# Splitting float64 weights with TensorE sums in a fused Fourier, channel-mix and expert kernel

## The chip, the cores and the metric

The kernel runs on one core of a Trainium2 chip. A core has five engines that take their instructions from queues of their own, in order: TensorE (PE, with its weight loads shown apart as PEld), VectorE (DVE), ScalarE (ACT), GpSimd (POOL) and SyncE (SP, which issues transfers here). The metric is the time of one execution in microseconds (us), the median of several runs.

## The reference

```
x = fft(fft(x, axis=1), axis=2).real                 # x: 4 x 3072 x 256, float32
x_prev = x one position back (zeros first)
xk = mu_k * x + (1 - mu_k) * x_prev ; xr likewise with mu_r
k = relu(xk @ w_k) ; v = (k * k) @ w_v ; r = sigmoid(xr @ w_r)
x = r * v                                            # w_k 256x1024, w_v 1024x256, w_r 256x256
# then a mixture of 8 experts over the 12288 rows, top one, capacity 384 each:
expert = argmax(x @ w_gate); the first 384 rows of each expert go through
y = relu(disp @ w1) @ w2, times the gate's weight; all other rows of the output are zero
```

`w_k`, `w_r` and `w_v` arrive as float64, because a float32 array was multiplied by a float64 scalar. The kernel gets them as pairs of 32-bit words and must make from them a high and a low part, whose three cross products stand for a float32 product on TensorE.

## The kernel before

The first batch goes through a two-dimensional Fourier transform before anything else can run ("the start"). It has three stages. Stage 1 has seven steps (`s1`): VectorE folds each step's inputs (four additions or subtractions), TensorE multiplies by a table in float32, ScalarE copies the result out of PSUM, and SP stores it to a scratch array `fd` in memory. `turn_round` then loads it back across partitions into tiles `tin` (`tload`, L362). Stage 2 (`s2`, L371) makes eight products from those tiles, stage 3 (`s3`, L397) eight more. Each leaves through ScalarE (L392, L418), and the stage 3 results through two or more VectorE operations (L428 to L436) into the transform `X`. Stages 2 and 3 are 16 units in a fixed order, 2 of stage 2 first and then alternating.

Beside the start stands the preparation of the weights: eight blocks of 128x512, five of `w_k` and `w_r` together and the rest three of four of `w_v`'s (`split64`, L762). Each block is loaded by SP as 512 KB of words, then takes four integer operations on VectorE (L769 to L772), an addition on GpSimd (L773), a copy to the high part (L774, on ScalarE, for `w_v` on VectorE) and a subtraction on GpSimd (L775). Between the units of stages 2 and 3 the loop in the main body runs three of these steps (`STEPS`); the rest of `w_v` is prepared in the first chunk (`more_v`, `VSTEPS`). Before stage 2, 36 matmuls on zeros keep TensorE running (`keep_warm`, `WARM`).

After that follow chunks of 512 positions (`chunk`, L624). A chunk has eight steps f: six matmuls of `mm_k` (L508), and from the fourth step on six of `mm_v` for the step three back, which reads block f // 2 of `w_v`. The third step also has the twelve matmuls of `mm_r`. ScalarE takes relu and square, and makes `kh` (L518, in chunk 0 for f < 4); VectorE makes `kl` (L519). What the matmuls read is made by `mix_part` (L463): ScalarE, VectorE, ScalarE, VectorE. The next batch's Fourier transform is spread over the chunks of the current one, from a plan written out by hand (`lay`, L954); the first two stage 1 steps of batch 1 are done in the start, in float32 (`EARLY`). All engines' orders are written out by hand, with no scheduler (`manual_schedule`).

At the end, the experts run.

Of the kernel before, what the change touches and what calls it, by code (L numbers as in the profile page):

```python
# [10 lines left out]
F32 = mybir.dt.float32  # L11
# [9 lines left out]
P = 128  # L21
# [82 lines left out]
def fourier_channel_mix_moe(  # L104
# [40 lines left out]

    tri = wts.tile([P, P], BF16, name="tri")
    ones = wts.tile([P, P], BF16, name="ones")
    gm = wts.tile([P, KD, P + E], F32, name="gm")
# [8 lines left out]
    d3 = [wts.tile([P, 2, 2, P], F32R, name=f"d3{h}") for h in range(2)]  # L157
    wk = [[wts.tile([P, KD, DFF], F32R, name=f"wk{f}{h}") for h in range(2)] for f in range(2)]
    wr = [[wts.tile([P, KD, D], F32R, name=f"wr{f}{h}") for h in range(2)] for f in range(2)]
    wv = [wts.tile([P, KF, D], F32R, name=f"wv{h}") for h in range(2)]  # L160
# [56 lines left out]
    def fft_buffers(pool, tag, nx, ns, nt, ng, nv, plain=False, keep=None):  # L217
# [19 lines left out]
        (s, w, d, h): fft.tile([P, CH], F32R, name=f"x{s}{w}{d}{h}")  # L237
        for w in range(2) for s in range(w + 1) for d in range(KD) for h in range(2)
    }


    def fft_units(b, bufs, table=None, between=lambda g: None, count=0, wait=0):

# [71 lines left out]
        def s1(j):  # L315
# [32 lines left out]

            later(wait, store) if wait and j < count else store()

# [20 lines left out]
        def s2(i):  # L371
            h = turns[i]
            ps = psm.tile([P, CH], F32, name="pm")
            w = UQ * HG * UC
            for t in range(2):
                for k in range(HG):
                    o = ps[:, w * t + UQ * UC * k:w * t + UQ * UC * (k + 1)]
                    z = h == 0 and k == 0
                    nc.tensor.matmul(
                        o, tins[i % NTI][:, k, t], m2[:, HG * h + k].rearrange("p u s -> p (u s)"),  # L380
                        start=True, stop=not z, skip_group_check=z,
                    )
# [11 lines left out]
            if i + NTI < NH:  # L394
                between(i + NTI)

# [47 lines left out]
        def turn_round():  # L444
            for g in range(NTI):
                tload(g)
            for g in range(NTI):
                between(g)

# [327 lines left out]

# [4 lines left out]

    def stage(k):
        raw = spare(k) if k < 2 else stg.tile([P, CH, 2], I32, name="raw", bufs=3)
        return raw, stg.tile([P, CH], I32, name="sa", bufs=3)

    def prep_r():
        src = words(ins["w_r"]).rearrange("(d p) n -> p d n", p=P)
        return split64(src, *(t.rearrange("p d n -> p (d n)") for t in wr[0]), *stage(4))

    def prep_k(d, h):
        src = words(ins["w_k"])[d * P:(d + 1) * P, 2 * CH * h:2 * CH * (h + 1)].rearrange("p (a n) -> p a n", a=1)
        return split64(src, *(t[:, d, CH * h:CH * (h + 1)] for t in wk[0]), *stage(2 * h + d))

    def prep_v(k):
        src = words(ins["w_v"])[2 * k * P:(2 * k + 2) * P].rearrange("(f p) n -> p f n", p=P)
        return split64(
            src, *(t[:, 2 * k:2 * k + 2].rearrange("p f n -> p (f n)") for t in wv),
            spare(k % 2), spare(2).rearrange("p n w -> p (n w)")[:, CH * (k % 2):CH * (k % 2 + 1)], nc.vector.tensor_copy,
        )  # L800

# [14 lines left out]
    with tc.manual_schedule():  # L816
        with tc.tile_pool(name="stg", bufs=2) as stg:
# [6 lines left out]
            def keep_warm(n):  # L824
# [17 lines left out]
            more["s"] = []  # L842
            pk = []

            preps = [
                lambda: prep_k(0, 0), lambda: prep_k(1, 0), prep_r,
                lambda: prep_k(0, 1), lambda: prep_k(1, 1), lambda: prep_v(0),
            ]

            held = []  # L850

            def prepare(steps):

                pk.extend(steps[:5] + held)
                held[:] = steps[5:]

            def between(g):
                if preps:
                    prepare(preps.pop(0)())

# [6 lines left out]
            )  # L867
            units = fft_units(0, more, t3, between, len(CSTEPS))
# [19 lines left out]
            )  # L888
            for k in ("mu_k", "mu_r"):
                v = ins[k].rearrange("(d o) -> d o", o=1)  # L890
                for d in range(KD):
                    nc.scalar.dma_start(mu[k, 0][:, d:d + 1], v[d * P:(d + 1) * P])
                    flipped(mu[k, 1][:, d:d + 1], v, d)
            do(units, len(CSTEPS))
            for u in range(UQ):
                rs = slice(2 * FC * u, 2 * FC * (u + 1))
                nc.scalar.dma_start(m2[rs, :, u], ins["c_m2"][rs].rearrange("r (g n) -> r g n", n=UC))
            nc.scalar.dma_start(mz, ins["c_mz"])
            nc.scalar.dma_start(t3.rearrange("p v t k -> p (v t k)"), ins["c_d3"])
            keep_warm(WARM)  # L900
            parts(d1, d1f)
            parts(d3, t3)
            units1 = fft_units(1, fbuf, None, lambda g: None, EARLY, 4)
            for n in range(len(units)):
                do(units)
                if n < 3:
                    keep_warm(2)
                do(pk, STEPS[n])
                if n == 13:
                    do(units1)  # L910
                if n == 10:
                    do(units1)
                    prepare(prep_v(1))
                    for k in ("mu_k", "mu_r"):
                        for f in range(2):
                            nc.vector.tensor_scalar(mu[k, f, 1], mu[k, f], -1.0, 1.0, op0=ALU.mult, op1=ALU.add)
# [8 lines left out]
            settle()  # L925
            do(pk, STEPS[-1])
            prepare(prep_v(2))
            pv = pk + held
# [3 lines left out]
            nc.sync.dma_start(ident, ins["c_ident"])  # L932
        mp = mix.enter_context(tc.tile_pool(name="mp", bufs=1))

        def more_v(f):
# [299 lines left out]
```

## Time and profile before

| what | value |
|---|---|
| time, median of 3 runs | 642.57 us (641.83 to 643.2) |
| the profiled execution's own time | 644.52 us |
| its span, first to last instruction | 642.7 us |
| mean granted TensorE clock | 0.957 |
| PE busy | 593.9 us, 92% |
| VectorE busy | 423.2 us, 66% |
| ScalarE busy | 353.1 us, 55% |
| GpSimd busy | 149.1 us, 23% |

The page's slices of 16 us, in tenths of busy time:

```profile
PE   5855889999999999999999999999988989999992
PEld 2553667888888888888788888889978989999992
DVE  5379899966666666699757665756665746655620
ACT  2131837666565656676556566566636745655630
POOL 7246256030202022240302030202221101111121
PEclk7877797999999999999999999999998989999997
DMA  7583598242108000152421061000107645555200
```

Each digit is the busy share of one of 40 equal slices; 9 is 90% or more. PEclk is the clock granted to TensorE. TensorE is full from the seventh slice on; the first six are the start and the first chunk.

### The profile page before, as it was taken

The numbers are of one execution on the slowest core, as the hardware profiler recorded it, in microseconds if no ns is written. First come the engines' busy times: TensorE is split into PE (matmuls) and PEld (weight loads), VectorE is DVE, ScalarE is ACT, GpSimd is POOL, SyncE is SP. The second block draws the span as 40 slices with busy tenths as digits, with TensorE's granted clock in tenths as the row PEclk, the third lists the DMA queues.
The fourth block names the chain that finished last, engine by engine and source line by source line (L and its number), as shares of the span: only waits on it lengthen the run. The fifth ranks groups of instructions, "written<-read, shape, count | busy, mean of one in ns | idle before, by whom it ended". The sixth has DMA issues, their size and how long they took to land. (4 is left out here: it accounts for less than half of the span.)

```text
span 642.7 us, 9640 instructions
## 1 busy us (share of the span) xinstructions
PE 593.9 (92%) x3386; PEld 516.9 (80%) x3387; DVE 423.2 (66%) x921; ACT 353.1 (55%) x685; POOL 149.1 (23%) x195
## 2 busy tenths in 40 slices
PE   5855889999999999999999999999988989999992
PEld 2553667888888888888788888889978989999992
DVE  5379899966666666699757665756665746655620
ACT  2131837666565656676556566566636745655630
POOL 7246256030202022240302030202221101111121
PEclk7877797999999999999999999999998989999997
DMA  7583598242108000152421061000107645555200
GB/s 241 154 252 111 161 337 287 86 154 93 61 15 291 1 25 11 60 163 101 134 93 36 9 208 48 7 1 3 56 11 236 213 149 181 161 161 173 66 26 26
DMA packets 57183, 73.98 MB, mean 115 GB/s; under 512 B 8020, under 2 KB 43073, under 8 KB 57126
## 3 DMA queue, kind: packets, MB, share of 16 engines
q1 hardware_dynamic: 48610, 59.46, 29.0%
q0 software_dynamic: 5936, 13.37, 6.3%
q10 hardware_dynamic: 2580, 0.44, 0.5%
q8 instruction: 29, 0.48, 0.3%
q14 instruction: 28, 0.23, 0.1%
HBM read 43.27 MB, written 33.91 MB: 120 GB/s over the span
## 5 line engine op out<-in xcount | busy, mean ns | idle before, releaser
L488 PE MATMUL pk<-x,wk 128*128 128x512 f32 (+2 forms) x672 | 172.0, 392 | 3.4 <-ACT x L211 3.0
L488 PEld LDWEIGHTS pk<-x,wk 128*128 128x128 f32 x672 | 120.5, 192 | 25.1 <-ACT x L211 3.3
L488 PE MATMUL pv<-kh,wv 128*128 128x512 f32 (+2 forms) x448 | 134.6, 382 | 1.1 <-issue 0.6
L180 POOL DMA_INDIRECT disp<-rows,slot x50 | 53.2, 1064 | 271.5 <-ACT tmp L478 87.4
L514 ACT ACTIVATE rk<-pk 128x512 f32<-128x512 f32 (+2 forms) x112 | 64.4, 575 | 86.5 <-PE pk L488 75.1
L518 DVE CAST kh<-rk 128x512 fp32r<-128x512 f32 (+2 forms) x108 | 46.5, 430 | 91.4 <-ACT rk L515 89.7
L488 PEld LDWEIGHTS pv<-kh,wv 128*128 128x128 f32 x448 | 83.0, 189 | 17.9 <-POOL wv L775 1.3
L488 PE MATMUL pv<-kl,wv 128*128 128x512 f32 (+2 forms) x224 | 85.6, 382 | 0.0
L519 DVE TENSOR_TENSOR kl<-rk,kh 128x512 fp32r<-128x512 f32 (+2 forms) x112 | 75.5, 674 | 5.7
L1136 PE MATMUL pd<-w,h 128*128 128x256 f32 x576 | 72.8, 283 | 0.0
L1136 PEld LDWEIGHTS pd<-w,h 128*128 128x128 f32 x576 | 72.0, 192 | 0.0
L515 ACT ACTIVATE rk<-rk 128x512 f32<-128x512 f32 (+2 forms) x112 | 68.2, 609 | 3.6
L1085 DVE TENSOR_TENSOR w<-raw,w 128x512 fp32r<-128x512 f32 x60 | 41.0, 685 | 41.4 <-ACT w L1084 41.4
L180 POOL DMA_INDIRECT out<-res,ids x24 | 23.6, 983 | 121.8 <-ACT res L1143 107.7
L488 PEld LDWEIGHTS pv<-kl,wv 128*128 128x128 f32 x224 | 42.4, 189 | 8.0
L1127 DVE SCALAR_TENSOR_TENSOR h<-pk,h 128x384 fp32r<-128x384 f32 x64 | 35.3, 551 | 14.7 <-ACT h L1126 14.5
L1143 ACT ACTIVATE res<-pd,g 128x256 f32<-128x256 f32 x24 | 11.4, 476 | 54.5 <-PE pd L1136 53.2
L211 ACT CAST x<-tmp 128x512 fp32r<-128x512 f32 (+2 forms) x56 | 32.7, 585 | 14.4 <-DVE tmp L479 14.2
L488 PE MATMUL pk<-x,wr 128*128 128x512 f32 (+2 forms) x168 | 38.7, 379 | 0.0
L1084 ACT CAST w<-raw 128x512 fp32r<-128x512 f32 x60 | 36.7, 613 | 0.0
L212 DVE TENSOR_TENSOR x<-tmp,x 128x512 fp32r<-128x512 f32 (+2 forms) x56 | 36.6, 656 | 0.0
L488 PEld LDWEIGHTS pk<-x,wr 128*128 128x128 f32 x168 | 30.7, 188 | 6.0
(184 smaller groups left out, 895.8 us busy)
## 6 DMA issues: line engine op xcount, KB each, us to landing
raw<-in_w SPq DMA_DIRECT2D x60, 256.0 KB
out<-blank SPq DMA_DIRECT2D x24, 512.0 KB
tin<-fd SPq DMA_DIRECT2D x22, 208.0 KB
xin<-in_x SPq DMA_DIRECT2D x15, 256.0 KB
fd<-f SPq DMA_DIRECT2D x14, 256.0 KB
disp<-blank SPq DMA_DIRECT2D x6, 530.0 KB
d<-disp SPq DMA_DIRECT2D x8, 397.5 KB
X<-in_w_v SPq DMA_DIRECT2D x4, 512.0 KB
```

Of the source, the lines that this page charges most:

```text
L180: i = nc.gpsimd.indirect_dma_start(out=dst, out_offset=bass.IndirectOffsetOnAxis(ap=idx, axis=0), in_=src, in_offset=None, bounds_check=la ...
L211: nc.scalar.copy(hl[0], src)
L212: later(n, lambda: nc.vector.tensor_tensor(hl[1], src, hl[0].bitcast(F32), op=ALU.subtract))
L488: nc.tensor.matmul(ps, w[a][:, k, m0:m0 + P], xs[c], start=(first and n == 0), stop=(last and n == 2),)
L514: nc.scalar.activation(r, ps, AF.Relu)
L515: nc.scalar.activation(r, r, AF.Square)
L518: nc.vector.tensor_copy(kh, r) if i or f > 3 else nc.scalar.copy(kh, r)
L519: nc.vector.tensor_tensor(kl, r, kh.bitcast(F32), op=ALU.subtract)
L1084: nc.scalar.copy(h, r)
L1085: nc.vector.tensor_tensor(l, r, h.bitcast(F32), op=ALU.subtract)
L1127: nc.vector.scalar_tensor_tensor(hl, ps, 0.0, hh.bitcast(F32), op0=ALU.max, op1=ALU.subtract)
L1136: nc.tensor.matmul(ps, hs[a][:, f, t * P:(t + 1) * P], w[c][:, f], start=(f == 0 and n == 0), stop=(f == KF2 - 1 and n == 2),)
```

## The change

Of each weight block the words now go through four VectorE operations, which leave a rounded-down float32 (`a`) and two words whose upper 16 bits are read as bf16. ScalarE copies `a` to the high part. TensorE sums four products into PSUM: the identity by `a` in float32, the negated identity by the high part, and two small multiples of the identity by the two bf16 views, whose columns lie 8 bytes apart. ScalarE copies the sum to the low part. GpSimd has no part in it. `first()` holds the VectorE operations and the copy, `rest()` the matmuls and the last copy.

The words of `w_k` and `w_r` are loaded from ScalarE's queue, one block after each of five steps of stage 1, and the stage 2 tables are loaded there too, after the third step. Two blocks are split before stage 2, between three runs of zeros (18, 6 and 10 matmuls); a third is begun there; that one and two more are finished beside stages 2 and 3. Eight `tin` tiles are held, so `turn_round` issues all eight loads at once. Of `w_v` the loads of two blocks are issued late in stage 3, the first is begun after the mixing, and all four are finished in chunk 0 at f = 1, 3, 4 and 6. Batch 1's first two stage 1 steps move into the chunks, with three products instead of a float32 one, and so do the mixing of `xr` for chunk 0 and the splitting of two Fourier tables. Some tiles lie in a pool that opens after the start.

```
-EARLY = 2
-STEPS = (4,) + (3,) * 11 + (3, 0, 0, 0, 0, 0, 2)
-VSTEPS = (2, 3, 4, 4, 4, 4, 4, 4)
-WARM = 36
+WARM = (18, 6, 10)
...
-    def split64(src, hi, lo, raw, a, copy=nc.scalar.copy):
-        nc.sync.dma_start(raw.rearrange("p (a n) w -> p a (n w)", a=src.shape[1]), src)
+    def split64(queue, pool, src, hi, lo, raw, a):
+        queue.dma_start(raw.rearrange("p (a n) w -> p a (n w)", a=src.shape[1]), src)
         lw, hw = raw[:, :, 0], raw[:, :, 1]
+        le, he = (raw.bitcast(BF16)[:, :, k] for k in (1, 3))
         v = a.bitcast(F32)
         vec = nc.vector
-        return [
-            lambda: vec.tensor_scalar(a, hw, 3, 0x3FFFFFF8, op0=ALU.logical_shift_left, op1=ALU.bitwise_and),
-            lambda: vec.scalar_tensor_tensor(hw, hw, -0x40000000, a, op0=ALU.bitwise_and, op1=ALU.bitwise_or),
-            lambda: vec.scalar_tensor_tensor(a, lw, 29, hw, op0=ALU.logical_shift_right, op1=ALU.bitwise_or),
-            lambda: vec.tensor_scalar(lw, lw, 28, 1, op0=ALU.logical_shift_right, op1=ALU.bitwise_and),
-            lambda: nc.gpsimd.tensor_tensor(a, a, lw, op=ALU.add),
-            lambda: copy(hi, v),
-            lambda: nc.gpsimd.tensor_tensor(lo, v, hi.bitcast(F32), op=ALU.subtract),
-        ]
+        def rest():
+            ps = pool.tile([P, CH], F32, name={id(psk): "pk", id(psm): "pm"}[id(pool)])
+            terms = (ident, v), (neg_i, hi), (ulp_i, le), (negulp_i, he)
+            for n, (w, y) in enumerate(terms):
+                nc.tensor.matmul(ps, w, y, start=(n == 0), stop=(n == len(terms) - 1), skip_group_check=True)
+            nc.scalar.copy(lo, ps)
+        def first():
+            vec.tensor_scalar(a, hw, 3, 0x3FFFFFF8, op0=ALU.logical_shift_left, op1=ALU.bitwise_and)
+            vec.scalar_tensor_tensor(a, hw, -0x40000000, a, op0=ALU.bitwise_and, op1=ALU.bitwise_or)
+            nc.scalar.copy(hi, v)
+            vec.tensor_scalar(hw, a, -0x800000, None, op0=ALU.bitwise_and)
+            vec.scalar_tensor_tensor(lw, lw, 9, hw, op0=ALU.logical_shift_right, op1=ALU.bitwise_or)
+        return first, rest
...
-            more = fft_buffers(stg, "a", 0, 0, 1, 2, 0, plain=True)
+            more = fft_buffers(stg, "a", 0, 0, NU // (UQ * HG) - len(fbuf["t"]), 2, 0, plain=True)
...
+            nc.scalar.dma_start(ident, ins["c_ident"])
...
-            keep_warm(WARM)
-            parts(d1, d1f)
-            parts(d3, t3)
-            units1 = fft_units(1, fbuf, None, lambda g: None, EARLY, 4)
+            behind = {
+                0: lambda: weights((0, 0)), 1: lambda: weights((1, 0)), 2: tables, 3: lambda: weights("r"),
+                4: lambda: nc.scalar.dma_start(t3.rearrange("p v t k -> p (v t k)"), ins["c_d3"]),
+                5: lambda: weights((0, 1)), 6: lambda: weights((1, 1)),
+            }
+            mus()
+            for j in range(len(CSTEPS)):
+                do(units)
+                behind.get(j, lambda: None)()
+            for t, k in ((neg_i, -1.0), (ulp_i, 2.0 ** -20), (negulp_i, -(2.0 ** -20))):
+                nc.scalar.activation(t, ident, AF.Copy, scale=k)
+            do(units)
+            pw[0, 0][0]()
+            keep_warm(WARM[0])
+            pw[0, 0][1]()
+            pw[1, 0][0]()
+            keep_warm(WARM[1])
+            pw[1, 0][1]()
+            keep_warm(WARM[2])
+            pw["r"][0]()
+            units1 = fft_units(1, fbuf)
+            beside = {
+                1: pw[0, 1][0], 3: pw["r"][1], 4: pw[1, 1][0], 6: pw[0, 1][1], 7: one_less_mu, 9: pw[1, 1][1],
+                10: lambda: pv.append(prep_v(0)), 11: lambda: pv.append(prep_v(1)), 12: lambda: do(units1),
+            }
             for n in range(len(units)):
                 do(units)
                 if n < 3:
                     keep_warm(2)
-                do(pk, STEPS[n])
+                beside.get(n, lambda: None)()
             settle()
             mix_part(0, 0)
             mix_part(0, 1)
-            do(units1, EARLY)
             settle()
-            do(pk, STEPS[-2])
-            mix_part(0, 2)
-            mix_part(0, 3)
+            pv[0][0]()
...
         def more_v(f):
-            do(pv, VSTEPS[f])
+            if f == 0:
+                parts(d1, d1f)
+                parts(d3, t3)
+            if f in (1, 3, 4, 6):
+                k = (1, 3, 4, 6).index(f)
+                pv[k][1]()
+                if k < 2:
+                    pv.append(prep_v(k + 2))
+                if k < 3:
+                    pv[k + 1][0]()
             if f == 1:
-                pv.extend(prep_v(3))
...
```

## Rows read from the trace of the kernel before

**Rows 1.** Windows: stretch, its length, busy us of PE, PEld, DVE, ACT, POOL; clock, DMA share, GB/s.
```profile
29.90:41.00 11.10, 4.85 (x37) 4.21 (x36) 5.67 (x9) 2.75 (x6) 1.33 (x1) 0.87 0.94 285
41.00:55.00 14.00, 10.21 (x56) 9.08 (x56) 13.72 (x25) 4.57 (x11) 8.75 (x8) 0.86 0.64 195
55.00:69.30 14.30, 8.23 (x20) 6.03 (x21) 13.55 (x26) 4.06 (x9) 9.09 (x8) 0.51 0.25 76
...
92.50:103.50 11.00, 7.63 (x20) 5.18 (x20) 10.41 (x17) 7.38 (x13) 5.62 (x4) 0.69 1.01 369
103.50:160.00 56.50, 55.87 (x305) 47.01 (x304) 44.98 (x97) 35.71 (x65) 12.58 (x18) 1.00 0.41 133
```
**Rows 2.** Timeline of TensorE: start us, us, engine, line, what, [idle before it and releaser].
```profile
15.15 1.10 PE L333 MATMUL pm<-X,d1f 128*128 128x258 f32 x4 [0.76 <-ACT tmp L344]
...
21.74 8.36 PE L828 MATMUL pk<-busy 128*128 128x512 bf16 x37
29.94 1.03 PE L379 MATMUL pm<-m,tin 128*128 128x100 f32 x8
...
41.05 2.00 PE L379 MATMUL pm<-m,tin 128*128 128x100 f32 x8 [6.30 <-DMA tin<-fd]
...
44.16 1.43 PE L379 MATMUL pm<-m,tin 128*128 128x100 f32 x8
...
47.21 0.84 PE L410 MATMUL pm<-Ga,rows 128*128 128x192 f32 x4
...
60.12 1.65 PE L410 MATMUL pm<-Ga,rows 128*128 128x192 f32 x4 [1.21 <-DVE X L428]
66.12 3.75 PE L333 MATMUL pm<-xin,d1f 128*128 128x258 f32 x8 [4.36 <-issue]
69.31 5.87 PE L488 MATMUL pk<-x,wk 128*128 128x512 f32 x18
...
92.54 0.63 PE L488 MATMUL pk<-x,wk 128*128 128x512 f32 x2
...
97.04 1.89 PE L488 MATMUL pk<-x,wk 128*128 128x512 f32 x3 [3.02 <-ACT x L211]
...
101.28 2.36 PE L488 MATMUL pk<-x,wk 128*128 128x512 f32 x6
103.47 0.62 PE L488 MATMUL pv<-kh,wv 128*128 128x512 f32 x2
...
107.60 2.91 PE L488 MATMUL pk<-x,wr 128*128 128x512 f32 x12
110.35 0.88 PE L333 MATMUL pm<-xsp,d 128*128 128x258 f32 x6
```
**Rows 3.** Groups by line, VectorE, 29.9 to 69.3 us: count, busy us, mean ns, idle before.
```profile
L770 DVE SCALAR_TENSOR_TENSOR raw<-raw,sa 128x512 int32<-128x512 int32 x3 | 4.4, 1469 | 0.1
...
L771 DVE SCALAR_TENSOR_TENSOR sa<-X 128x512 int32<-128x512 int32 x2 | 1.4, 693 | 0.1
L772 DVE TENSOR_SCALAR raw<-raw 128x512 int32<-128x512 int32 x3 | 1.3, 428 | 0.1
```
**Rows 4.** Groups by line, GpSimd, the same stretch.
```profile
L775 POOL TENSOR_TENSOR wk<-sa,wk 128x512 fp32r<-128x512 f32 x4 | 5.9, 1479 | 0.0
```
**Rows 5.** Timeline of ScalarE's and SP's work and queues at four places.
```profile
22.01 4.08 ACTq L897 DMA_DIRECT2D m<-in_c_m  x4
...
66.13 0.32 ACT L418 COPY oa<-pm 128x192 f32<-128x192 f32 x1 [5.62 <-DVE X L434]
...
74.72 0.59 ACT L514 ACTIVATE rk<-pk 128x512 f32<-128x512 f32 x1
...
78.21 6.81 SPq L941 DMA_DIRECT2D disp<-blank  x6
```
**Rows 6.** Windows of stage 1 (columns of rows 1).
```profile
2.75:13.75 11.00, 6.43 (x16) 3.39 (x15) 6.31 (x12) 1.17 (x2) 9.35 (x26) 0.71 0.94 316
13.75:25.00 11.25, 8.82 (x33) 4.95 (x33) 6.89 (x16) 2.62 (x5) 3.94 (x20) 0.83 0.35 126
```

More of the change, by code (lines that the diff above doesn't have):

```diff
@@ L146, in fourier_channel_mix_moe @@
     tri = wts.tile([P, P], BF16, name="tri")
+    neg_i = wts.tile([P, P], F32R, name="neg_i")
+    ulp_i, negulp_i = (wts.tile([P, P], BF16, name=f"ulp{k}") for k in range(2))
     ones = wts.tile([P, P], BF16, name="ones")
@@ L157, in fourier_channel_mix_moe @@
     d3 = [wts.tile([P, 2, 2, P], F32R, name=f"d3{h}") for h in range(2)]
-    wk = [[wts.tile([P, KD, DFF], F32R, name=f"wk{f}{h}") for h in range(2)] for f in range(2)]
-    wr = [[wts.tile([P, KD, D], F32R, name=f"wr{f}{h}") for h in range(2)] for f in range(2)]
+    wk = [[wts.tile([P, KD, DFF], F32R, name=f"wk0{h}") for h in range(2)]]
+    wr = [[wts.tile([P, KD, D], F32R, name=f"wr0{h}") for h in range(2)]]
     wv = [wts.tile([P, KF, D], F32R, name=f"wv{h}") for h in range(2)]
@@ L237, in fourier_channel_mix_moe, with late_buffers, fft_units @@
         (s, w, d, h): fft.tile([P, CH], F32R, name=f"x{s}{w}{d}{h}")
-        for w in range(2) for s in range(w + 1) for d in range(KD) for h in range(2)
+        for s, w in ((0, 1),) for d in range(KD) for h in range(2)
     }
-    def fft_units(b, bufs, table=None, between=lambda g: None, count=0, wait=0):
+    def late_buffers(pool):
+        for w, n, name in ((wk, DFF, "wk"), (wr, D, "wr")):
+            w.append([pool.tile([P, KD, n], F32R, name=f"{name}1{h}") for h in range(2)])
+        for s, w in ((0, 0), (1, 1)):
+            for d in range(KD):
+                for h in range(2):
+                    xbuf[s, w, d, h] = pool.tile([P, CH], F32R, name=f"x{s}{w}{d}{h}")
+    def fft_units(b, bufs, table=None, count=0):
         xv = x[b].rearrange("(a c) n -> a c n", c=NC)
@@ L347, in store @@
                 nc.sync.dma_start(fd[:, place[j]:place[j] + n], f)
-            later(wait, store) if wait and j < count else store()
+            store()
         def load_zero():
@@ L781, in spare, with half @@
         return sp[:, 2 * CH * k:2 * CH * (k + 1)].rearrange("p (n w) -> p n w", w=2)
-    def stage(k):
-        raw = spare(k) if k < 2 else stg.tile([P, CH, 2], I32, name="raw", bufs=3)
-        return raw, stg.tile([P, CH], I32, name="sa", bufs=3)
+    def half(k):
+        return spare(2).rearrange("p n w -> p (n w)")[:, CH * k:CH * (k + 1)]
     def prep_r():
         src = words(ins["w_r"]).rearrange("(d p) n -> p d n", p=P)
-        return split64(src, *(t.rearrange("p d n -> p (d n)") for t in wr[0]), *stage(4))
+        hl = (t.rearrange("p d n -> p (d n)") for t in wr[0])
+        return split64(nc.scalar, psk, src, *hl, stg.tile([P, CH, 2], I32, name="raw", bufs=1), stg.tile([P, CH], I32, name="sa", bufs=3))
     def prep_k(d, h):
         src = words(ins["w_k"])[d * P:(d + 1) * P, 2 * CH * h:2 * CH * (h + 1)].rearrange("p (a n) -> p a n", a=1)
-        return split64(src, *(t[:, d, CH * h:CH * (h + 1)] for t in wk[0]), *stage(2 * h + d))
+        raw = stg.tile([P, CH, 2], I32, name=f"raw{d}{h}", bufs=1)
+        return split64(
+            nc.scalar, psk, src, *(t[:, d, CH * h:CH * (h + 1)] for t in wk[0]), raw, stg.tile([P, CH], I32, name="sa", bufs=3)
+        )
     def prep_v(k):
         src = words(ins["w_v"])[2 * k * P:(2 * k + 2) * P].rearrange("(f p) n -> p f n", p=P)
[L797 to L800, printed above, removed]
+        hl = (t[:, 2 * k:2 * k + 2].rearrange("p f n -> p (f n)") for t in wv)
+        return split64(nc.sync, psm, src, *hl, spare(k % 2), half(k % 2))
     def flip_weights():
@@ L842, in fourier_channel_mix_moe @@
             more["s"] = []
[L843 to L859, printed above, removed]
             one = len(CSTEPS) - 2
@@ L867, in fourier_channel_mix_moe @@
             )
-            units = fft_units(0, more, t3, between, len(CSTEPS))
+            units = fft_units(0, more, t3, len(CSTEPS))
             do(units, 2)
             keep_warm(8)
+            nc.scalar.dma_start(ident, ins["c_ident"])
             nc.gpsimd.iota(neg, pattern=[[-P, KD]], base=D, channel_multiplier=-1)
@@ L888, in fourier_channel_mix_moe @@
             )
[L889 to L897, printed above, removed]
@@ L898, in fourier_channel_mix_moe, with tables @@
-            nc.scalar.dma_start(mz, ins["c_mz"])
-            nc.scalar.dma_start(t3.rearrange("p v t k -> p (v t k)"), ins["c_d3"])
-            keep_warm(WARM)
-            parts(d1, d1f)
-            parts(d3, t3)
-            units1 = fft_units(1, fbuf, None, lambda g: None, EARLY, 4)
+            def tables():
+                for u in range(UQ):
+                    rs = slice(2 * FC * u, 2 * FC * (u + 1))
+                    nc.scalar.dma_start(m2[rs, :, u], ins["c_m2"][rs].rearrange("r (g n) -> r g n", n=UC))
+                nc.scalar.dma_start(mz, ins["c_mz"])
@@ new lines, in mus, with weights @@
+            def mus():
+                for k in ("mu_k", "mu_r"):
+                    v = ins[k].rearrange("(d o) -> d o", o=1)
+                    for d in range(KD):
+                        nc.scalar.dma_start(mu[k, 0][:, d:d + 1], v[d * P:(d + 1) * P])
+                        flipped(mu[k, 1][:, d:d + 1], v, d)
+            pw = {}
+            def weights(*ks):
+                for k in ks:
+                    pw[k] = prep_r() if k == "r" else prep_k(*k)
+            behind = {
[3 more added lines that the diff above has]
+            }
@@ new lines, in fourier_channel_mix_moe, with one_less_mu @@
+            pw["r"][0]()
+            units1 = fft_units(1, fbuf)
+            def one_less_mu():
+                for k in ("mu_k", "mu_r"):
+                    for f in range(2):
+                        nc.vector.tensor_scalar(mu[k, f, 1], mu[k, f], -1.0, 1.0, op0=ALU.mult, op1=ALU.add)
+            beside = {
+                1: pw[0, 1][0], 3: pw["r"][1], 4: pw[1, 1][0], 6: pw[0, 1][1], 7: one_less_mu, 9: pw[1, 1][1],
+                10: lambda: pv.append(prep_v(0)), 11: lambda: pv.append(prep_v(1)), 12: lambda: do(units1),
+            }
@@ L904, in fourier_channel_mix_moe @@
+            pv = []
             for n in range(len(units)):
@@ L907, in fourier_channel_mix_moe @@
                     keep_warm(2)
-                do(pk, STEPS[n])
[L909 to L916, printed above, removed]
+                beside.get(n, lambda: None)()
             settle()
```

10 lines of the change are left out of this document (1 added, 9 removed).

## The prediction, made before the changed kernel ran

> **What bounds the kernel now.** I read the windows by stretch first, then TensorE's timeline, then the other engines where TensorE waits. From 103.5 us on TensorE is busy 55.87 of 56.50 us at clock 1.00 [rows 1]: a shift of what goes before moves the end by as much, and a matmul added there costs its own time. Before that it is not the bound. From 29.9 to 69.3 it is busy 4.85 of 11.10, 10.21 of 14.00 and 8.23 of 14.30 us, while VectorE is busy 13.72 of 14.00 and 13.55 of 14.30 from 41 on [rows 1]. So the start has two limits in turn: a transfer (TensorE waits 6.30 us until 41.05 for a `tin` tile [rows 2], while DMA is 0.94 busy [rows 1]), then VectorE. A third loss is at the seam of chunks 0 and 1: the stretch from 92.5 has TensorE 7.63 of 11.00 us busy at clock 0.69, VectorE 10.41 of 11.00 [rows 1]; TensorE waits 3.02 us before 97.04 for the mixing, and runs slow until 103.47 [rows 2].
>
> Why VectorE is full: an integer operation over two tensors takes 693 ns where nothing disturbs it (L771), but L770 on `raw` takes 1469 ns on average [rows 3]. GpSimd's subtraction, 1479 ns long [rows 4], runs beside it. Undisturbed, a block is 2 x 693 + 2 x 428 = 2.24 us of VectorE.
>
> **Units of cost.** Twelve matmuls of 512 columns go from 107.60 to 110.35: 0.229 us each at clock 1.00; their row is 2.91 long, so a lone tail is 0.16 [rows 2]. A stage 1 step in float32 has 512 columns in all and takes 1.10 us [rows 2], 0.94 without its tail. A weight sum is one such product and three of 0.229: 1.63 us. The two bf16 views are strided by 8 bytes, which no row shows: at least 0.229 each as the other products, at most 0.47, the half of the float32 step's 0.94, the slowest 512 columns of one pass in the rows; that would add 0.5 to each sum. I take 0.229, as TensorE here takes one column at a time at the same pace for 4-byte data.
>
> **The change, part by part.**
>
> *Up to stage 2.* Stage 1 ends at 21.74, and TensorE then runs zeros until 29.94 [rows 2]. Now come 34 matmuls (7.8 us) and two sums (3.3 us): stage 2 starts at 32.8, **+2.9**. What must be ready by then: the words of the two blocks, loaded from 7 us on; VectorE's 4.5 us for them, which start when its folds end near 21; three small ScalarE operations for the new identities; the `tin` tiles. The table loads, 4.08 us of ScalarE's queue [rows 5], now stand between two of its stage 1 copies. TensorE has three PSUM buffers to run on, and ScalarE, free from 19.7 instead of 15.0, has 4 copies and 4 issues left, so the last store leaves some 0.6 us late; cover: 11.1 us of zeros and sums. Its cost is nothing to 2 us. The added five clearings of `tin` are GpSimd's while it is idle; it waits on the folds until 21 for its next work.
>
> *Stages 2 and 3.* Eight `tin` loads leave before any weight word that SP used to issue among them, so the 6.30 us wait goes; GpSimd leaves, and VectorE has 2 blocks (4.5 us) and the stage 3 results in this stretch instead of 6 disturbed blocks. What is late next is TensorE itself. Four units take from 44.16 to 48.05 [rows 2], 0.97 each: 16 make 15.6. Add 6 zeros (1.4), three sums (4.9) and half a block of VectorE in front of a stage 3 result (1.2): 23.1 us, to 55.9. Before, the last unit ended at 60.12 + 1.65 = 61.77 [rows 2].
>
> *To the first chunk.* From the last copy of stage 3 (66.13 [rows 5]) to the first matmul of chunk 0 (69.31 [rows 2]) are 3.2 us, with a hand-over 3.5. The fold and the two float32 steps of batch 1 (3.75 us of TensorE [rows 2]), which stood there, are gone. Chunk 0 starts at 59.4 instead of 69.31: **-9.9** for all so far.
>
> *Chunk 0.* It took 92.54 - 69.31 = 23.2 us [rows 2]. Now: its 90 matmuls at 0.229 (20.6); four sums (6.5); a slow beginning after 3.5 us of idleness, 1.6 as now (18 matmuls in 5.7 us, not 4.1 [rows 2]); and waits. In the first four steps ScalarE and VectorE are the late ones. Say that chunk 0 starts at T. Behind the mixing VectorE owes two low parts and two operations (2.5 us) before ScalarE can make the first high part of `w_v`, at T + 2.7, where TensorE would want it at about T + 2.4: 0.9 us with the hand-overs. Then ScalarE has 7 operations near 0.6 us (the 0.59 of L514 [rows 5]) with the tables and the mixing for `xr`, which were done before, then 4 for step 0 and a sum; the next high part waits for VectorE until T + 10.9, and the relu of step 1 behind it ends at T + 12.1. TensorE wants that PSUM buffer for the second half of `mm_r` at T + 9.6: 2.5 us. In sum 32.1 us, **+8.9**. The bounds of the waits are 0 (if the hand-overs run better) and 6. The words of the third block go ahead of the six blank stores, those of the fourth behind their 6.81 us of issue [rows 5] and behind the second sum: they land near T + 17, and TensorE wants their sum at T + 25: hidden.
>
> *Chunk 1.* The wait came from VectorE, which was held by GpSimd. Its work in chunk 0 is now some 21 of 32 us, and the mixing for chunk 1 stands late in the chunk. The 18 matmuls that went from 92.54 to 103.47 [rows 2] take 4.1: **-6.8**. Two steps of batch 1 are added, in three products (0.88 us for six matmuls [rows 2]): **+1.8**. Stores, issues and folds that move with them lie beside a full TensorE.
>
> Sum: -9.9 + 8.9 - 6.8 + 1.8 = -6.0 us. Against the profiled execution's own 644.52 us that is 638.5; the median of the runs shown is 642.57, 1.95 lower, and gives **636.6 us**.
>
> **The rivals.**
> *The sums are nearly free.* ScalarE keeps up in chunk 0 and TensorE stays fast after the shorter start: without the waits (3.4), the slow beginning (1.6) and the 1.2 us of VectorE, 630.4 us. For it: ScalarE is idle in most of 29.9 to 69.3 [rows 1]. Against: its order in chunk 0 is fixed, and the mixing now stands in it.
>
> *The words take the start's transfers.* Between 2.75 and 13.75 us DMA is 0.94 busy, from then to 25 it is 0.35 [rows 6]. Five blocks are 2.6 MB, at the 369 GB/s of the chunk seam [rows 1] 7.1 us. If all of it went ahead of the Fourier rows, stage 2 would start at 29.9 + 7.1 = 37.0, 4.2 us behind my 32.8, and after an idle stretch as long as that before 97.04 TensorE would run slow as there (15 matmuls in 6.4 us instead of 3.4 [rows 2]): +7.2, so 643.8. Against it: the free DMA time from 13.75 to 25, 0.65 x 11.25 = 7.3 us, holds just these bytes. The Trainium skill (Trainium Kernel Development and Optimization, Key Constraints) has the rule: transfers from the SP, ACT and POOL queues run on the same 16 DMA engines and interleave, so that another queue saves only issue time. By that rule the words are not free for being on ScalarE's queue; no row of before has two such large streams at once. By it the time would be this rival's 643.8, without it my sum.
>
> *The other side: each sum stops TensorE.* The sums stand in TensorE's queue before the step's `mm_k`, and its order is fixed. If the high part comes some 3 us late at each of f = 1, 3, 4 and 6, because ScalarE's copy stands behind relu, square and low part, the stop brings a slow stretch too: 3.0 idle and 3.0 lost at the lower clock, as at 97.04 [rows 2]. I count one stop without a slow stretch. With its slow stretch (3.0) the gain is down to 3; with one stop more it is gone (+3), with two more it is +9: 651.6 us. It decides from the second stop. Against it: from the fourth step on a step has 12 matmuls (2.75 us) for three to five ScalarE operations, and the high part is ordered one step or two ahead.
>
> **How the numbers follow.** My forecast 0.54, nearly free 0.20, the transfers 0.12, stops 0.14. About 0.2% (1.3 us) is what a measurement can tell from no change. The forecast's own range is 632 to 642, of which 0.04 is within 0.2%; of the transfers' 0.12 I put 0.05 faster, 0.04 same, 0.03 slower. Faster 0.50 + 0.20 + 0.05 = 0.75; same 0.08; slower 0.14 + 0.03 = 0.17. The range is 629 to 645: it takes in the strided reads at their dearest (9 sums x 0.5 = 4.5), the waits' upper bound, most of the first two rivals, and leaves out the stops.
>
> **What would show it.** Stage 2's first product near 33 us with no wait for `tin`; DVE below 60% and TensorE's clock near 1.00 from 33 to 56; chunk 0's first matmul near 59; one stop of TensorE of 2 to 3 us before the second half of `mm_r`; sums 1.6 us long; no wait at the start of chunk 1. I am wrong if stage 2 waits for `tin` or a table past 35, if the sums wait for their high part at f = 3, 4 or 6, or if VectorE is still full when chunk 1 starts.

## The result and the profile after

| what | before | after |
|---|---|---|
| median of 7 runs each | 643.2 us (641.63 to 645.0) | 637.09 us (635.57 to 638.16, and one run of 858.35) |
| ratio after / before, 95% interval | | 0.9900 (0.9879 to 0.9922) |
| profiled execution: time, span | 644.52, 642.7 us | 636.79, 635.1 us |
| mean granted TensorE clock | 0.957 | 0.984 |
| GpSimd busy | 149.1 us | 126.8 us |

The change makes the kernel 6.1 us faster by the medians; by the interval it is 5.0 to 7.8. I had forecast 6.0. The run of 858.35 us, at a granted clock of 0.66, is in a slow state and is left out of the ratio; without it the median is 636.94. The two profiles differ by more, 7.6 us of span, and not all of that is the change, as shown below.

The windows of the profile after (stretch, length, busy us of PE, PEld, DVE, ACT, POOL; clock, DMA share, GB/s), to be laid beside [rows 1]:

```profile
32.80:45.00 12.20, 12.15 (x75) 9.10 (x74) 3.67 (x12) 5.70 (x12) 2.57 (x7) 1.00 0.96 319
45.00:56.00 11.00, 9.99 (x56) 7.64 (x55) 3.40 (x14) 4.59 (x11) 0.00 (x0) 1.00 0.03 9
...
62.00:95.00 33.00, 30.70 (x119) 21.36 (x119) 22.23 (x39) 25.16 (x45) 6.37 (x6) 1.00 0.92 293
95.00:105.00 10.00, 9.64 (x45) 7.67 (x44) 9.65 (x17) 6.82 (x13) 5.13 (x5) 1.00 0.53 174
```

In stages 2 and 3 TensorE is now full at clock 1.00, and VectorE is busy a third of the time. The stretch that was slow at the seam of chunks 0 and 1, here from 91.4 us on, has no loss left.

TensorE's timeline after, the lines that answer to [rows 2]:

```profile
22.68 4.76 PE L847 MATMUL pk<-busy 128*128 128x512 bf16 x17
27.27 1.02 PE L784 MATMUL pk<-sa,ident 128*128 128x512 f32 x2
27.73 0.79 PE L784 MATMUL pk<-wk,neg_i 128*128 128x512 f32 x1
28.37 1.06 PE L784 MATMUL pk<-raw,ulp 128*128 128x512 bf16 x2
29.25 1.48 PE L847 MATMUL pk<-busy 128*128 128x512 bf16 x6
...
34.71 1.03 PE L387 MATMUL pm<-m,tin 128*128 128x100 f32 x8
...
52.91 2.37 PE L416 MATMUL pm<-Ga,rows 128*128 128x192 f32 x12
58.70 2.93 PE L492 MATMUL pk<-x,wk 128*128 128x512 f32 x6 [3.43 <-ACT x L210]
...
70.12 1.66 PE L492 MATMUL pk<-x,wr 128*128 128x512 f32 x6 [2.30 <-ACT rk L518]
...
91.38 1.53 PE L492 MATMUL pk<-x,wk 128*128 128x512 f32 x6
...
99.62 2.91 PE L492 MATMUL pk<-x,wr 128*128 128x512 f32 x12
...
124.61 0.74 PE L341 MATMUL pm<-xsp,d 128*128 128x258 f32 x4 [2.03 <-DVE xsp L211]
```

Read it against the forecast: stage 2 begins at 34.71 with no wait, chunk 0 at 58.70 after 3.43 us of idleness, TensorE stops once in `mm_r` (2.30), chunk 1 begins at 91.38 without a wait. New is the wait of 2.03 us before 124.61, for VectorE (a second one of 0.85 us follows before 129.19).

Where the time came from, by marks that both traces have: the first matmul of chunk 0, the first matmul of `mm_r` in later chunks, and the experts' down products (`y`'s second matmul):

| mark | before | after | shift |
|---|---|---|---|
| first matmul of chunk 0 | 69.31 | 58.70 | -10.6 |
| `mm_r`, chunk 1 | 107.60 | 99.62 | -8.0 |
| `mm_r`, chunk 2 | 138.89 | 135.29 | -3.6 |
| `mm_r`, chunk 11 | 440.15 | 436.78 | -3.4 |
| first down product of the experts | 494.5 | 491.1 | -3.4 |
| last down product | 631.0 | 623.3 | -7.7 |

The last 4.3 us come in the experts, which the change does not touch. There TensorE waited for the rows `d` in the profile before; this is the waits view (waited for: total us, times, longest us) of the kernel before:

```profile
PE pm L1108 <- DMA d<-disp: 2.6, 1, 2.6
```

After has no such wait. Behind it TensorE ran slow for a while: from 490 to 530 us its granted clock was 0.96, in after 1.00. The wait (2.6) and that slow stretch (0.04 of 40 us, 1.6) make up the 4.3.

### The profile page after: what moved, and what is told of

Read it like the earlier page. It is cut to its first block, busy times and chain, and to the rows that moved or that the text cites. A ratio compares the mean times of both kernels' runs of the same rounds, so it can differ in the third digit from the quotient of the medians.

```text
span 635.1 us, 9732 instructions
## 1 busy us (share of the span) xinstructions
PE 600.8 (95%) x3430; PEld 517.0 (81%) x3434; DVE 408.6 (64%) x919; ACT 362.6 (57%) x703; POOL 126.8 (20%) x182
## 5 line engine op out<-in xcount | busy, mean ns | idle before, releaser
L492 PEld LDWEIGHTS pk<-x,wk 128*128 128x128 f32 x672 | 119.2, 190 | 25.3 <-ACT x L210 3.7
L518 ACT ACTIVATE rk<-pk 128x512 f32<-128x512 f32 (+2 forms) x112 | 64.4, 575 | 82.0 <-PE pk L492 80.5
L523 DVE TENSOR_TENSOR kl<-rk,kh 128x512 fp32r<-128x512 f32 (+2 forms) x112 | 74.4, 665 | 10.4 <-ACT kh L522 4.8
L1162 DVE SCALAR_TENSOR_TENSOR h<-pk,h 128x384 fp32r<-128x384 f32 x64 | 35.3, 552 | 13.4 <-ACT h L1161 7.9
L210 ACT CAST x<-tmp 128x512 fp32r<-128x512 f32 (+2 forms) x56 | 32.7, 585 | 5.9 <-DVE tmp L483 5.5
```

The lines of the kernel that those rows point to most:

```text
L210: nc.scalar.copy(hl[0], src)
L492: nc.tensor.matmul(ps, w[a][:, k, m0:m0 + P], xs[c], start=(first and n == 0), stop=(last and n == 2),)
L518: nc.scalar.activation(r, ps, AF.Relu)
L523: nc.vector.tensor_tensor(kl, r, kh.bitcast(F32), op=ALU.subtract)
L1162: nc.vector.scalar_tensor_tensor(hl, ps, 0.0, hh.bitcast(F32), op0=ALU.max, op1=ALU.subtract)
```

## The experiments

All ratios are to the kernel before, run beside them on the same chip. Compare them with after's 0.9900 (0.9879 to 0.9922).

**1. The kernel before once more** (no edit).

> The kernel before, unchanged, once more with a profile. From the start of the experts' down products (494.5) to their last (631.0) the profile before took 136.5 us, with a wait of 2.65 us for the rows d; five profiles of kernels with the same expert part took 132.2 to 134.7. If the wait belongs to the way transfers happen to land, this profile has another length (132 to 135) and chunk 11 still has its mm_r near 440. If it belongs to the old kernel's order, 136 to 137 again.

644.95 us, one run. Chunk 11 has its `mm_r` at 441.99, and the down products go from 497.2 to 631.5, 134.3 us. The wait for `d` is there again and shorter:

```profile
PE pm L1108 <- DMA d<-disp: 1.8, 1, 1.8
```

So the wait varies from one execution to the next. Whether the old order makes it longer is not settled: the four profiles with the old order have it at 1.0 to 2.6 us, the ten with the new one at 0 to 2.2, and four of these not at all. The 4.3 us of the experts can therefore not be counted as the change's, nor all as chance. By this profile the shift at chunk 11 is 441.99 - 436.78 = 5.2 us, by the first one 3.4.

It shows something else: here TensorE never waits for `tin` in stage 2, and yet chunk 0 starts no sooner:

```profile
71.08 4.94 PE L488 MATMUL pk<-x,wk 128*128 128x512 f32 x18
```

The wait of 6.30 us [rows 2], which I had taken for the first limit of the start, was not one.

**2. Only the word loads moved, in the kernel before.**

```
-        nc.sync.dma_start(raw..., src)
+        (nc.sync if copy is nc.vector.tensor_copy else nc.scalar).dma_start(raw..., src)
...
+            for j in range(len(CSTEPS)):       # stage 1 steps
+                do(units)
+                if j in behind:                # {0: k00, 1: k10, 3: r, 5: k01, 6: k11}
+                    prepare(behind[j]())
```

> The kernel before with only the five word loads of w_k and w_r moved into stage 1, on ScalarE's queue; the split stays on VectorE and GpSimd. My theory, two limits in turn: the wait for tin until 41.05 goes and VectorE can begin at 30 instead of 35.8, but its six disturbed blocks still take 20 us, so chunk 0 starts 4 to 6 us sooner (63 to 65) and the time is 637 to 640. Rival one, VectorE and GpSimd alone set the start: less than 2 us. Rival two, the loads alone do: chunk 0 at 60 or sooner, as in the changed kernel.

645.54 us, ratio 1.0036 (1.0015 to 1.0057): slower. TensorE's timeline of this kernel, with one of its windows (columns as above):

```profile
36.26 2.00 PE L379 MATMUL pm<-m,tin 128*128 128x100 f32 x8 [4.00 <-DMA mz<-in_c_mz]
...
72.26 4.66 PE L488 MATMUL pk<-x,wk 128*128 128x512 f32 x18
```
```profile
55.00:70.00 15.00, 8.02 (x22) 6.07 (x23) 14.72 (x27) 2.80 (x9) 10.18 (x9) 0.51 0.30 94
```

The words delayed the tables, which here are loaded after stage 1; stage 2 began 6.3 us later than before, and chunk 0 only 3 us later, behind a VectorE busy 14.72 of 15.00 us. No wait for `tin` is left and nothing is gained, so my expectation missed and the time is that of rival one. But this run does not test early words by themselves. In the old order VectorE's first block stands behind the splitting of two Fourier tables (L212), which waits for ScalarE and that for the tables. VectorE's timeline at its first block, in the kernel before, in experiment 1, in this kernel (the last splitting and the block) and in the changed one:

```profile
35.82 0.43 DVE L769 TENSOR_SCALAR sa<-X 128x512 int32<-128x512 int32 x1 [2.52 <-DMA X<-in_w_k]
```
```profile
36.98 0.69 DVE L212 TENSOR_TENSOR d<-rows,d 128x512 fp32r<-128x512 f32 x1 [6.84 <-ACT d L211]
37.58 0.42 DVE L769 TENSOR_SCALAR sa<-X 128x512 int32<-128x512 int32 x1
```
```profile
37.89 0.69 DVE L212 TENSOR_TENSOR d<-rows,d 128x512 fp32r<-128x512 f32 x1 [2.53 <-ACT d L211]
38.50 0.42 DVE L770 TENSOR_SCALAR sa<-X 128x512 int32<-128x512 int32 x1
```
```profile
21.27 0.42 DVE L788 TENSOR_SCALAR sa<-raw 128x512 int32<-128x512 int32 x1
```

| old order | VectorE's first block | chunk 0 | between |
|---|---|---|---|
| before | 35.82 | 69.31 | 33.5 |
| experiment 1 | 37.58 | 71.08 | 33.5 |
| experiment 2 | 38.50 | 72.26 | 33.8 |
| experiment 5 | 46.43 | 79.88 | 33.5 |

From VectorE's first operation on a block to chunk 0 it is 33.5 to 33.8 us, whatever TensorE waited for in stage 2. In the profile before, the six blocks take 19.9 us of that, where six undisturbed ones would take 6 x 2.24 = 13.4. So the start before does have two limits in turn, a transfer and then VectorE; but the transfer is the one for which VectorE's first block waits (words in the profile before, a table in experiments 1 and 2), not `tin`. Early words gained nothing here because the table came late. In the changed kernel the splitting of the tables stands in chunk 0, the words are there, and VectorE begins 14.5 us sooner than before.

**3. Words late, in the changed kernel.**

```
-                0: lambda: weights((0, 0)), 1: lambda: weights((1, 0)), 2: tables, 3: lambda: weights("r"),
+                2: tables,
...
-                5: lambda: weights((0, 1)), 6: lambda: weights((1, 1)),
...
             do(units)                          # turn_round
+            weights((0, 0), (1, 0), "r", (0, 1), (1, 1))
             pw[0, 0][0]()
```

> The changed kernel with all five word loads of w_k and w_r issued from ScalarE's queue behind stage 1, not within it. My theory: stage 1 is 0.5 to 1 us shorter, but the first sums wait for words that land near 28, stage 2 starts at 36 to 38 instead of 34.7, and the time is 1 to 3 us longer (638 to 640). Rival, the words in stage 1 cost more than they give, since the last store of stage 1 took 6.8 us to be ready for reading instead of 2.75: stage 2 starts sooner than 34.7 and the time falls under 636.

647.04 us, ratio 1.0077 (1.0057 to 1.0098): the whole gain and more is gone: some 11 us, where I had expected 1 to 3. TensorE's timeline of this kernel:

```profile
31.42 2.08 PE L784 MATMUL pk<-sa,ident 128*128 128x512 f32 x2 [4.15 <-DVE sa L789]
37.04 0.79 PE L784 MATMUL pk<-wk,neg_i 128*128 128x512 f32 x1 [3.54 <-ACT wk L790]
...
45.12 1.03 PE L387 MATMUL pm<-m,tin 128*128 128x100 f32 x8
```

The first words land at 30.2, and the sum stands in TensorE's queue ahead of stage 2, so stage 2 begins at 45.12, 10.4 us later. The second stop, for the high part, I had not thought of: ScalarE's queue was busy with the last two word loads from 30.21 to 36.32, and only then made it. So the early loads are a condition of the sums before stage 2.

**4. Three stage 2 inputs instead of eight, in the changed kernel.**

```
-            more = fft_buffers(stg, "a", 0, 0, NU // (UQ * HG) - len(fbuf["t"]), 2, 0, plain=True)
+            more = fft_buffers(stg, "a", 0, 0, 1, 2, 0, plain=True)
```

> The changed kernel with three stage 2 inputs held instead of eight. My theory: with the words loaded in stage 1 nothing stands ahead of the refills, so each arrives in time or up to 1 us late: the same within 2 us (637 to 639). Rival, eight held inputs are what shortened the start: waits for tin of 5 us or more come back, 642 or more.

637.23 us, ratio 0.9924 (0.9903 to 0.9945): the same within the measurement. Chunk 0 starts at 58.63, and TensorE waits for no `tin`. The eight inputs are worth nothing measurable here.

**5. Eight inputs alone, in the kernel before** (`1` becomes `6` in the line above, two flipped weights in the later pool). Since `between` then runs for all blocks at once, all word loads leave together, and the sixth takes the place of the first block's words before these are split: part of `w_k` is other data here.

> The kernel before, with only the eight stage 2 inputs held at once (two flipped weight tiles moved to the later pool to make room). My theory: the 6.3 us wait for a tin tile goes, but VectorE with its six disturbed blocks stays full from 41 us on and sets the start of chunk 0: at most 2 us sooner than 69.3, time 640 to 643. Rival, the transfers are what made the start long: chunk 0 begins 5 us or more sooner and the time falls to 637 or less. Beside that: TensorE's wait of 2.65 us for the expert rows d (some 523 us in the profile before) should show again if it belongs to the old kernel, and be absent if it was chance.

652.26 us, ratio 1.0159 (1.0136 to 1.0182). Not the experiment that I meant: TensorE waited 13.75 us for ScalarE's copy L392, which stood behind a high part of such a block. It says nothing on the eight inputs. It does give a point to the table of experiment 2: VectorE's first block began 10.6 us late and so did chunk 0. On the experts it says that the old order can have a wait of 1.0 us.

**6. `w_v`'s low parts by GpSimd, in the changed kernel** (the last bits of `w_v` left out).

```
+        def rest_gp():
+            nc.gpsimd.tensor_tensor(lo, v, hi.bitcast(F32), op=ALU.subtract)
+        rest = rest_gp if pool is psm else rest_pe
```

> The changed kernel with the low parts of w_v made by one GpSimd subtraction each instead of a TensorE sum (the last bits of w_v, which the sum adds, are left out). It takes four sums of 2 us off TensorE in chunk 0 and brings four GpSimd operations back beside VectorE. My theory, VectorE disturbed by GpSimd is what made the seam wait: VectorE's two-input operations beside them take 1.4 us or more, and part of the 8 us is lost again in waits of chunk 0 or at the seam: 632 to 637. Rival, the sums are pure cost in chunk 0: the whole 8 us comes, 629 or less.

635.2 us, ratio 0.9899 (0.9874 to 0.9923): the same, with four sums off TensorE. Its timeline in chunk 0:

```profile
57.79 7.17 PE L492 MATMUL pk<-x,wk 128*128 128x512 f32 x18 [3.43 <-ACT x L210]
...
70.19 2.58 PE L492 MATMUL pk<-x,wr 128*128 128x512 f32 x6 [2.60 <-ACT rk L518]
```

The second half of `mm_r` begins at 70.19; in the changed kernel, with the sums, it is 70.12. Up to there the chain of VectorE and ScalarE sets the time and the sums fill waits. By `mm_r` of chunk 1 the kernel is 3.9 us ahead (95.73), of which a wait for `d` takes 2.2 later. The number is in my range, the reason was not borne out: no wait came back at the seam. VectorE's and GpSimd's timelines show how little they met:

```profile
60.69 0.69 DVE L797 SCALAR_TENSOR_TENSOR X<-X 128x512 int32<-128x512 int32 x1
61.30 1.50 DVE L211 TENSOR_TENSOR d<-d1f,d 128x256 fp32r<-128x256 f32 x1
```
```profile
60.93 1.59 POOL L788 TENSOR_TENSOR wv<-X,wv 128x512 fp32r<-128x512 f32 x1 [23.96 <-ACT wv L795]
```

At all four subtractions the block's last operation (L797) was already running and kept its 693 ns. The one operation over two tensors that began beside one took 1505 ns; in the changed kernel it takes 0.42 us. So the disturbance is there, but four subtractions do not bring the seam's wait back; which of the things taken from VectorE and GpSimd removed it (the disturbance, the copies of `w_v`'s high parts, the later place of the blocks) stays open.

**7. Fewer zeros before stage 2** (`WARM = (18, 6, 2)`).

> The changed kernel with 26 matmuls on zeros before stage 2 instead of 34 (18, 6 and 2). In the profile after, stage 2's first product starts at 34.71 us, at once behind the last zeros. My theory: the zeros and the two sums, not the transfers, set that start now, so it comes 1 to 1.7 us sooner and the time falls by as much (635.4 to 636.2). Rival, the tin tiles and the zeroed tile land at 34 anyway, behind the words: the start moves less than 0.5 us and the time stays.

639.6 us, ratio 0.9935 (0.9911 to 0.9960); in its profile chunk 0 begins at 61.03, 2.3 us later than after's. The timeline:

```profile
25.66 1.02 PE L784 MATMUL pk<-sa,ident 128*128 128x512 f32 x2
...
33.00 1.11 PE L387 MATMUL pm<-m,tin 128*128 128x100 f32 x8 [1.46 <-DMA tz<-fd]
...
34.96 0.55 PE L387 MATMUL pm<-m,tin 128*128 128x100 f32 x2 [0.42 <-DMA tin<-fd]
...
38.29 1.87 PE L387 MATMUL pm<-m,tina 128*128 128x100 f32 x8
```

Stage 2 starts 1.7 us sooner, but 1.6 of that stand already at the first sum (25.66 for 27.27), ahead of the zeros that were taken out. From there it is 7.3 us for 7.4: the zeros became a wait for `tz`, a small tile that is loaded with `tin`. In that the rival is right. TensorE waits twice and then runs at the lower clock (0.51 from 35 to 42 us, in after 1.00): eight products take 1.87 us instead of 1.03. Neither theory had that. The zeros seem worth their time; the intervals of the two ratios still touch.

**8. The second `w_v` block begun one step later** (`pv[1][0]()` at f = 2).

> The changed kernel with the second w_v block's VectorE operations and its high copy ordered one step later (at f = 2 instead of f = 1). My theory: TensorE's wait of 2.3 us in the second half of mm_r comes from the relu of step 1, which stands behind that copy on ScalarE; it shrinks under 1 us and 1 to 2 us are saved (635 to 636). Rival, ScalarE has too much work there in any order: the wait stays or moves to the sum at f = 3, and the time stays.

638.26 us, ratio 0.9925 (0.9905 to 0.9945): no gain. The 2.3 us stop in `mm_r` goes, and the sum at f = 3 waits 1.06 us instead, for a block of VectorE's that stands behind a 1.60 us wait for ScalarE's `kh`; the start of chunk 0 runs slow for longer, and `mm_r` of chunk 1 is at 99.19 for 99.62. The rival is right.

**9. Word results in contiguous tiles.**

```
-        le, he = (raw.bitcast(BF16)[:, :, k] for k in (1, 3))
+        le, he = (y.bitcast(BF16).rearrange("p (n w) -> p n w", w=2)[:, :, 1] for y in (p0, p1))
...
-            vec.tensor_scalar(hw, a, -0x800000, None, op0=ALU.bitwise_and)
-            vec.scalar_tensor_tensor(lw, lw, 9, hw, ...)
+            vec.tensor_scalar(p1, a, -0x800000, None, op0=ALU.bitwise_and)
+            vec.scalar_tensor_tensor(p0, lw, 9, p1, ...)
```

> The changed kernel with the two word results of each block written to contiguous tiles, so that the bf16 views have columns 4 bytes apart instead of 8. In the profile after, each of the two bf16 products takes 0.44 us instead of 0.23, a sum 1.98 us instead of my 1.63. My theory: the stride costs it, and at 4 bytes the products take 0.23: sums of 1.55 us, some 3 us less over the seven sums that TensorE is waiting through nothing else for (634 to 635). Rival, any stride of bf16 costs as much, or it is not the stride: sums stay at 2 us and the time stays.

634.8 us, ratio 0.9878 (0.9855 to 0.9901). One sum in its timeline:

```profile
25.66 1.02 PE L786 MATMUL pk<-sa,ident 128*128 128x512 f32 x2
26.11 0.80 PE L786 MATMUL pk<-wk,neg_i 128*128 128x512 f32 x1
26.75 0.62 PE L786 MATMUL pk<-ps,ulp 128*128 128x512 bf16 x2
27.21 1.46 PE L849 MATMUL pk<-busy 128*128 128x512 bf16 x6
```

From the first line to the last, 1.55 us; in the profile after, 27.27 to 29.25, 1.98. The two bf16 products take 0.46 together instead of 0.88. The stride was it. By the mark in chunk 11 the profile is 3.8 us ahead of after's (433.01), but 1.6 of them stand already at its first sum (25.66 for 27.27), ahead of what the edit changes; by the ratios it is 1.4 us (0.9900 - 0.9878), and their intervals overlap. Stage 2 waits 0.52 us for `tz` here, until 32.90.

**10. Batch 1's steps spread three steps sooner** (`FIRST = 2`).

> The changed kernel with batch 1's Fourier steps spread from the sixth step of chunk 0 on, three steps sooner. In the profile after, TensorE waits 2.03 and 0.85 us between 122 and 130 us for VectorE's low part of a stage 1 input, a cost that I had not counted. My theory: VectorE has too much in chunks 1 and 2, and room in chunk 0, so the waits shrink by 2 us or more (634 to 635.5). Rival, the waits move to other places of a VectorE that is as full: same time.

644.85 us, ratio 1.0020 (0.9999 to 1.0040): the gain is lost. VectorE's and GpSimd's timelines of this kernel:

```profile
120.00 0.69 DVE L302 TENSOR_TENSOR dif<-xin,xre 128x512 f32<-128x512 f32 x1 [5.49 <-DMA xre<-in_x,mir]
```
```profile
104.30 0.99 POOL L171 DMA_INDIRECT wk<-flip,neg  x1 [14.62 <-ACT x L210]
...
115.76 1.00 POOL L278 DMA_INDIRECT xre<-in_x,mir  x1 [0.30 <-DMA wk<-flip,neg]
```

The next input's mirrored half is loaded by GpSimd, behind eight loads of flipped weights that take it from 104.3 to 115.8. VectorE waited 5.49 us for it and TensorE 4.17 us for VectorE's routing. Both theories had left out GpSimd's queue.

**11. The two early steps back in the start.**

```
-            units1 = fft_units(1, fbuf)
+            units1 = fft_units(1, fbuf, None, 2)
...
             mix_part(0, 1)
+            do(units1, 2)
             settle()
```

> The changed kernel with batch 1's first two stage 1 steps back in the start, in float32, behind the mixing for chunk 0. From mm_r of chunk 1 to mm_r of chunk 2 the changed kernel takes 35.67 us and the kernel before 31.29: 4.4 us, where I had counted 1.8 for the two steps. My theory: the two steps are what overfills VectorE there, so 3 to 4.4 us come back, and in the start they lie in the 3.4 us in which TensorE waits: 633 to 635.5. Rival, they cost as much in the start (fold on VectorE, slow clock, ScalarE's copies): same time within 1 us.

636.42 us, ratio 0.9898 (0.9881 to 0.9915): the same. From chunk 1's `mm_r` to chunk 2's are 134.82 - 102.25 = 32.6 us instead of 35.7, so 3.1 come back, and the start gives 2.1 of them away:

```profile
58.35 2.05 PE L341 MATMUL pm<-xin,d1f 128*128 128x258 f32 x4 [2.17 <-DVE X L434]
60.76 1.65 PE L492 MATMUL pk<-x,wk 128*128 128x512 f32 x3 [0.36 <-ACT x L210]
```

The steps do lie in the idle stretch, but slow and in two pieces, and chunk 0 begins at 60.76. The rival holds.

**12. Experiments 9 and 11 together.**

> Both the contiguous word results (columns of the bf16 views 4 bytes apart) and the two early steps. If the two gains are of different places they add: 3 us from the sums, and what the early steps give: 630 to 632.5. If both fill the same wait (ScalarE in chunk 0), no better than the better of the two.

634.18 us, ratio 0.9859 (0.9836 to 0.9881): the fastest version that was run, and short of the 630 to 632.5 that I expected. By the mark in chunk 11 it is 4.4 us ahead of after's (432.34), near the sum of the two alone (3.8 and 0.9). Its interval lies below that of the kernel before and just overlaps with after's, so against the changed kernel it is likely, not settled.

## Why the prediction was right, step by step

- *Up to stage 2*, +2.9 forecast, +4.8 measured (34.71 for 29.94). Mis-sized: stage 1 ended at 22.68 instead of 21.74 (in experiment 1 the kernel before ended it at 22.50, so this part is no more than executions differ), and each of the two sums took 1.98 us instead of 1.63. No transfer was waited for. Stage 1's last store left at 23.32 and the first `tin` load at 30.13, 6.8 us later, where before it was 22.52 and 25.27; the zeros and sums hid that. It is the words that make it: in experiment 2, where only they are moved, it is 6.7 us (23.75 to 30.48), in experiment 1 2.1. The Trainium skill's rule (Trainium Kernel Development and Optimization, Key Constraints) that transfers of all queues share the engines agrees with these 6.8 us; the time that I gave for it, 643.8, did not come. The cover is thin: with fewer zeros or cheaper sums stage 2 waits until 33.00 and 32.90 (experiments 7 and 9).
- *The sum.* I took the strided bf16 products at 0.229 and kept 0.47 as the other end. It was 0.44, at the dear end. The Trainium skill (SBUF — State Buffer, Door 1: The DMA port swizzle) gives full bandwidth to accesses that hit the same 16-byte line and asks for at least two hits per line, which would make a step of 8 bytes free for bf16. Here TensorE's read at that step took twice the time, and at 4 bytes full pace; the measurement decides.
- *Stages 2 and 3*, 23.1 us forecast, 34.71 to 55.28 = 20.6 measured, dearer sums included. A unit took 0.67 to 0.87 us, not 0.97: the row that I took it from lies in a stretch where TensorE's clock was 0.86 [rows 1]. VectorE held up nothing. This error cancels the first step's: chunk 0 at 58.70, forecast 59.4.
- *Chunk 0*, +8.9 forecast, 91.38 - 58.70 = 32.7 for 23.2: +9.5. The stop before the second half of `mm_r` is where I had put it and as long (2.30 for 2.5); ScalarE's timeline after shows its cause, the second `w_v` high part (L790) waiting for VectorE, with the relu of step 1 (L518) behind it:

```profile
67.04 0.58 ACT L785 CAST wv<-pm 128x512 fp32r<-128x512 f32 x1
68.96 0.62 ACT L790 CAST wv<-X 128x512 fp32r<-128x512 f32 x1 [1.34 <-DVE X L789]
69.48 0.59 ACT L518 ACTIVATE rk<-pk 128x512 f32<-128x512 f32 x1
```

- *The seam*, -6.8 forecast and measured: 91.38 to 95.50 for what took 92.54 to 103.47. That the wait goes was right; that GpSimd's disturbance alone had made it was not shown (experiment 6).
- *The two moved steps*, +1.8 forecast, 35.67 - 31.29 = +4.4 measured: the term that failed. I counted TensorE's time and wrote that folds and stores lie beside a full TensorE. VectorE was full there instead, busy 14.03 of 15.00 us from 120 to 135, and TensorE waited 2.03 and 0.85 us for its low parts. Experiment 11 gives 3.1 of it back.
- *What bounds the kernel.* My first limit, TensorE's wait for `tin`, was none (experiments 1, 2 and 4): the transfer that came first was the one in front of VectorE's first block, and the second limit, VectorE, was right. The start is shorter because VectorE's work in it begins 14.5 us sooner (21.27 for 35.82), is undisturbed (693 ns for L789 after, where L770 took 1469 [rows 3]), and is less: four blocks are done before stage 2 and one beside stages 2 and 3, where there were six. The early words are needed for that. How much each of the three gives no run separates.
- *The experts*, nothing forecast, -4.3 between the two profiles: one wait and the slow stretch behind it, whose length varies; how much of it is the change's stays open.

So the 6.0 of the forecast met the 6.1 of the medians with the sum up to the experts at -3.4 in one pair of profiles and -5.2 in the other; that the total fits so well is in part luck. Of the rivals none came true in its time: the sums are not free over the chunk, the words did delay the first `tin` load by 4.9 us but were covered, and TensorE stopped once, not at each sum.

## What to carry to other kernels

A wait that stands in the timeline need not be a limit: before it is counted as a gain, ask whether the engine behind it would have been late anyway, when that engine could begin, and look at a second profile. Work that is moved beside a full engine needs each of its instructions placed on the queues that are already full there; here that was VectorE, and in another order GpSimd's queue. Before the products of a strided operand are counted at full pace, the step should be measured: here 8 bytes halved the pace of bf16 and 4 bytes did not.

## What the runs showed of the hardware that I had not expected

- 512 bf16 columns took 0.44 us at a step of 8 bytes and 0.23 at 4 bytes, at the same granted clock of 1.00 (after and experiment 9).
- A float32 product of 512 columns, as two records, and the float32r product behind it took 1.10 us (27.27 to 28.37 after); with 0.23 for the second, an estimate from the other float32r products, the first took 0.87.
- Behind two short waits (1.46 and 0.42 us) eight products took 1.87 us instead of 1.03, at a granted clock of 0.51 from 35 to 42 us (experiment 7).
- A VectorE operation over two tensors that began while GpSimd's subtraction ran took 1505 ns, one of its kind that was already running the usual 693 (experiment 6).
- The same four table loads occupied ScalarE's queue 4.08 us [rows 5] and, behind two word loads, 7.95 us (experiment 2).
